# A fused attention-and-MLP kernel: reordering the second and third row chunk of its first phase

## The chip, the cores and the metric

The kernel runs on one core of one Trainium2 chip. The metric is the device time of one execution in microseconds (us). Engines are named as the profile names them: PE (TensorE, matmuls), PEld (its weight loads), DVE (VectorE), ACT (ScalarE), POOL (GpSimd), SP (SyncE, which here issues most transfers).

## The reference

For 2048 rows of width 512, the result mixes a linear attention `a` and an MLP `b` by a gate. All of it is float32.

```python
x = A_x                                              # 1 x 2048 x 512
g = sigmoid((x * gate_w).sum(-1, keepdims=True))
qkv = x @ wqkv                                       # 32 heads of 16
pq, pk = q @ w_phi[h], k @ w_phi[h]                  # per head, 16 x 16
phi = concat([softmax(p), softmax(-p)], -1)          # features, 32 per head
kv = einsum("bhsf,bhsd->bhfd", phi_k, v)             # summed over all rows
z  = einsum("bhsf->bhf", phi_k)
a  = ((phi_q @ kv) / (phi_q . z + 1e-6)) @ wo
h  = x @ w1 + b1                                     # 1376 hidden
b  = (h * tanh(softplus(h))) @ w2
out = g * a + (1 - g) * b
```

## The kernel before, in words

**Precision.** A float32 product is made of three products of split operands: each operand is written as a high part (rounded to PE's fp32r) and a low part (operand minus high part). ScalarE makes the high part by a copy, VectorE or GpSimd makes the low part by a subtraction. So every weight and every block of x costs a copy and a subtraction, and every matmul group is `xh·wh`, `xh·wl`, `xl·wh`.

**Stages.** A start stage multiplies the per-head matrices `w_phi` into the K and Q weights (`fuse`, into PSUM) and splits the results into `wkh`, `wkl`, `wqh`, `wql` (`fsplit`, L806); `raw_k` (L821) also copies the unsplit K weights out, since differences of them are needed later. The K products of the first chunk are woven into this stage (`k_part`, L813). Phase A then goes through the 2048 rows in 8 chunks of 256 rows (`a_ops`, two tiles of 128 rows each). Phase B does the MLP and the rest of the attention in 4 blocks of 512 rows.

**A chunk of phase A.** `k`, `v`, `q` are PE's groups of 12 matmuls a tile. VectorE turns K into features: `mx` and `mn` (largest and smallest of each head), `d0` and `d1` (two subtractions into the tile `E`), then ScalarE's exponential `E`, then VectorE's sum `S`, reciprocal `rS` and multiplication `ml` (L292). `ve` and `qe` are ScalarE's evictions of V and Q, `st` stores Q's projection. `z` adds the features into a sum in DRAM by an accumulating transfer on GpSimd's queue. `kv` (L455) multiplies the features with V and adds into one PSUM tile for all chunks; it needs `ml` and `ve` of both tiles. `xh` and `xl` split x of the next chunk, `ldx` loads x of the chunk after that.

**Fast chunks.** Chunks 3 and 4 counted from 0 (the fourth and fifth) use fewer products, made of sums of weights (`t1` to `t4`, L301) and sums of x (`sa`, split by `sh` and `sl`). The sums of weights are split by the steps `h0` to `h3` (ScalarE) and `l0` to `l3` (GpSimd, `l2` VectorE). In a fast chunk `ca` (L376) adds two products in PSUM on VectorE before the group `s4` continues it. The names `H`, `O`, `L` with a number are the copy, subtraction and load of a piece of the MLP's weights.

**Order.** Nothing is scheduled by the compiler around these steps: every engine does its instructions in the order of the program. That order is written by hand as strings, one for each chunk: `FIRST`, `SECOND` and `BEFORE` for chunks 0, 1 and 2, `SEVEN` for the fast ones, and so on. `run` (L209) takes the names one after another and issues each step on its engine. A plain name is a step of the chunk itself, `'` one of the chunk before, `+` one of the chunk after, `#` a weight step. Each engine has its own queue, so the order in a string matters only between steps of one engine, and through the waits between engines.

**Buffers.** The feature tiles `E` have 4 buffers, V tiles (`io`) 4, x in raw form (`tx`) 2, split x (`hl`) 8 half-tiles. PSUM has 3 tiles for K and Q (`a`), 4 for V and others (`dn`), one for `kv`. A step that takes a buffer waits until its last reader is done.

Of the kernel before, what the change touches and what calls it, by code (L numbers as in the profile page):

```python
# [34 lines left out]
FAST = range(3, 5)  # L35
# [6 lines left out]
    S0 rS0 ml0 S1 rS1 ml1 q0 qe0 st0 q1 qe1 st1  # L42
"""
SECOND = """
    h0# h1# l0# h3# l1# l3# z0' z1' k0 xh mx0 mn0 d00 d10 xl ldx k1 E0 L0# L1# mx1 mn1 d01 d11 v0 E1 S0 rS0 ve0 ml0 t2# h2# z0
    v1 S1 rS1 ml1 ve1 q0 qe0 st0 q1 qe1 st1 l2# kv' kv
"""
BEFORE = """
    k0 z1' xh xl sa mx0 mn0 d00 d10 ldx k1 E0 H0# O0# L2# mx1 mn1 d01 d11 v0 E1 sh0 sl0 S0 rS0 ve0 ml0 z0
    v1 H1# O1# L3# S1 rS1 ml1 ve1 q0 qe0 st0 q1 sh1 sl1 qe1 st1  # L50
"""
SEVEN = """
# [46 lines left out]
def tile_gated_mix(ctx: ExitStack, tc: tile.TileContext, xT, wv, wkT, wqT, bd, w1a, w1b, b1, w2a, w2b, wo, out):  # L99
# [10 lines left out]
    def mm(*a, **k):  # L110
        return pin(nc.tensor.matmul(*a, **k))  # L111
# [8 lines left out]
    def k4(name, tag, dt=F32):  # L120
        return T([P, 1024], dt, tag, {"E": 4, "tx": 2, "oh": 2, "z": 1}[tag], name)

    def k2(name, tag, dt=F32):
        return T([P, 512], dt, tag, {"pq": 3, "io": 4, "hl": 8}[tag], name)
# [5 lines left out]
    def act(out_, in_, fn=AF.Copy, **k):  # L130
        return pin(A_.activation(out_, in_, fn, **k))  # L131
# [7 lines left out]
    def f32(ap):  # L139
        return ap.bitcast(F32)  # L140
# [65 lines left out]
    def at(key, name, fn):  # L206
        steps.setdefault((key, name), []).append(fn)
# [32 lines left out]
    def proj(x, t, wh, wl, tag):  # L240
        ps = psum("proj", tag)
        xh, xl = x
        sl = slice(t * P, (t + 1) * P)
        n = 0
        for a, w in ((xh, wh), (xh, wl), (xl, wh)):
            for k in range(KT):
                mm(ps, a[k // 2][:, k % 2, sl], w[:, k, :], start=(n == 0), stop=(n == 3 * KT - 1))
                n += 1
        return ps
# [10 lines left out]
    def feat_ops(key, t, src, d, negative=False):  # L260

        n = str(t)

        def red(name, op):
            d[name] = T([P, H], F32, name, 2, name)
            pin(V.tensor_reduce(d[name], hv(src()), axis=AX.X, op=op))

        def dd(a):
            if "E" not in d:
                d["E"] = k4("E", "E")  # L270
            E = hv(d["E"][:, a * 512 : (a + 1) * 512])
            if (a == 0) != negative:
                pin(V.tensor_sub(E, hv(src()), d["mx"][:, :, None].to_broadcast([P, H, DH])))
            else:
                ins = pin(V.tensor_sub(E, d["mn"][:, :, None].to_broadcast([P, H, DH]), hv(src())))  # L275
                if key == ("B", 0) and t == 1:
                    last[0] = ins

        def ss():
            d["S"] = T([P, 2 * H], F32, "Sm", 2, "Sm")  # L280
            pin(V.tensor_reduce(d["S"], hv(d["E"][:, :]), axis=AX.X, op=ALU.add))  # L281

        at(key, "mx" + n, lambda: red("mx", ALU.max))
        at(key, "mn" + n, lambda: red("mn", ALU.min))
        at(key, "d0" + n, lambda: dd(0))
        at(key, "d1" + n, lambda: dd(1))
        at(key, "E" + n, lambda: act(d["E"], d["E"], AF.Exp))
        at(key, "S" + n, ss)
        at(key, "rS" + n, lambda: pin(V.reciprocal(d["S"], d["S"])))

    def scale_by(d, eng):
        pin(eng.tensor_mul(hv(d["E"][:, :]), hv(d["E"][:, :]), d["S"][:, :, None].to_broadcast([P, 2 * H, DH])))  # L292
# [96 lines left out]
    def a_ops(c):  # L389
        key = ("A", c)  # L390
        P_ = psA[c] = {}
        for t in range(2):
            d = {}
            Es[c, t] = d

            def k_(t=t):
                P_["k", t] = proj(xs[c], t, wkh, wkl, "a")

            def v_(t=t):
                P_["v", t] = proj(xs[c], t, wvh, wvl, "dn" if c or t else "kv")  # L400

            def q_(t=t):
                P_["q", t] = proj(xs[c], t, wqh, wql, "a")

            def ve(t=t):
                vs[c, t] = k2("v", "io")
                act(vs[c, t], P_["v", t])

            def qe(t=t):
                P_["qs", t] = k2("qs", "pq")  # L410
                act(P_["qs", t], P_["q", t])

            def qa(t=t):
                P_["qs", t] = k2("qs", "pq")
                pin(V.scalar_tensor_tensor(P_["qs", t], P_["q", 0], -1.0, P_["m7s"], op0=ALU.mult, op1=ALU.subtract))

            def st(t=t):
                i = 2 * c + t
                pin(Sy.dma_start(pqd[i * P : (i + 1) * P, :], P_["qs", t]))

            at(key, f"v{t}", v_)
            if c not in FAST:
                at(key, f"k{t}", k_)
                at(key, f"q{t}", q_)
            at(key, f"ve{t}", ve)
            if t and c in FAST:
                at(key, "qa", qa)
            else:
                at(key, f"qe{t}", qe)
            at(key, f"st{t}", st)  # L430
            feat_ops(key, t, lambda t=t: P_["k", t][:, :], d, t == 1 and c in FAST)
            at(key, f"ml{t}", lambda d=d: scale_by(d, V))

            def zs(t=t, d=d):
                if c >= NCH - 2:
                    end = c == NCH - 1
                    for sl in (slice(0, 512), slice(512, 1024)) if end and t else (slice(0, 1024),):
                        ins = pin(G_.tensor_add(Z["acc"][:, sl], Z["acc"][:, sl], d["E"][:, sl]))
                        if end and not sl.start:
                            tc.add_manual_dep(ins.ins, last[t].ins.name, SYNC, reason="VectorE's own sums first")  # L440
                elif c:
                    pin(G_.dma_start(zd[t][:, :], d["E"], accum_op=ALU.add))
                else:
                    pin(G_.dma_start(zd[t][:, :], d["E"]))

            at(key, f"z{t}", zs)
        if c == NCH - 2:
            def zld():
                Z["acc"] = k4("zacc", "z")
                pin(Sy.dma_start(Z["acc"], zd[0][:, :]))  # L450

            at(key, "zld", zld)
            at(key, "za", lambda: pin(G_.dma_start(Z["acc"], zd[1][:, :], accum_op=ALU.add)))

        def kv():  # L455
            if not kvs:
                kvs.append(psum("kvp", "kv")[:, : NG * 64].rearrange("p (g f) -> p g f", g=NG))
            (kvp,) = kvs
            for t in range(2):
                E, v = Es[c, t]["E"], vs[c, t]  # L460
                Ev = E[:, :].rearrange("p (a r b x) -> p b r a x", a=2, r=2, b=8)
                for u in range(8):
                    for r in range(2):
                        o = (u % 2) * 64 + 32 * r
                        mm(kvp[o : o + 32, u // 2, :], v[:, u * 64 + 32 * r : u * 64 + 32 * r + 32], Ev[:, u, r, :, :],
                           start=(c == 0 and t == 0 and u < 2), stop=(c == NCH - 1 and t == 1), skip_group_check=True)

        odd = c + 1 - c % 2
        if odd + 1 in FAST:
            at(("A", odd + 1), "kk", kv)  # L470
        else:
            at(key, "kv", kv)
        if c in FAST:
            fast_ops(c, key, P_)
        if c + 1 in FAST:
            fast_operands(c + 1, key)
        if c + 1 < NCH:
            def xh():
                new_x(c + 1)
                for j in range(2):  # L480
                    x_hi(c + 1, j)

            at(key, "xh", xh)
            for j in range(2):
                at(key, "xl", lambda j=j: x_lo(c + 1, j, V if c else G_))
        if c + 2 < NCH:
            at(key, "ldx", lambda: ldx(c + 2))
# [318 lines left out]
    def fsplit(h, l, k):  # L806
        act(h[:, k, :], acc[k])
        pin(V.tensor_sub(l[:, k, :], acc[k], f32(h[:, k, :])))
# [4 lines left out]
    def k_part(k):  # L813
        for t in range(2):
            sl = slice(t * P, (t + 1) * P)
            if t not in pk:
                pk[t] = psum("proj", "a")
            for n, (a, w) in enumerate(((xs[0][0], wkh), (xs[0][0], wkl), (xs[0][1], wkh))):
                mm(pk[t], a[k // 2][:, k % 2, sl], w[:, k, :], start=(k == 0 and n == 0), stop=(k == KT - 1 and n == 2))

    def raw_k(k):  # L821
        act(wkr[:, k, :], acc[k])
# [7 lines left out]
    fsplit(wkh, wkl, 1)  # L830
    acc[2] = fuse(skT, 2)
    fsplit(wkh, wkl, 2)
    raw_k(0)
    raw_k(1)
    k_part(0)
    acc[3] = fuse(skT, 3)
    fsplit(wkh, wkl, 3)
    k_part(1)
    for j in range(2):
        h, l = [w[:, 2 * j : 2 * j + 2, :].rearrange("p k f -> p (k f)") for w in (wvh, wvl)]  # L840
# [99 lines left out]
```

## Time and profile before

| | |
|---|---|
| median of 3 runs | 457.06 us (456.77 to 458.35) |
| the profiled execution | 457.48 us |
| its span, first to last instruction | 455.6 us |
| PE, DVE, ACT, POOL busy | 444.9, 318.3, 207.1, 153.7 us |
| granted TensorE clock, mean | 0.996 |

The profile page is that of one execution. Its waits name the engine whose event came last; a timeline row gives the start, the duration, the engine, the line, what is written from what, how many instructions are merged into the row and, in brackets, the idle time before it with what ended it. Helper lines such as L111 (matmul) and L131 (ScalarE) stand for many steps, so rows are told apart by tiles: `proj<-wkh,xh` is a K group, `wvh` V, `wqh` Q. The tiles named `th`, `tl`, `sh`, `sl` written from `wkr` or `wqr` are the split sums of weights. The third chunk's K group starts at 54.18 us, the fourth chunk's first group at 71.62 us.

### The profile page before, as it was taken

Reading aid. Unit: us, or ns where it says so; the run is one execution under the profiler, and the core shown is the slowest. Engines: PE = TensorE matmul, PEld = TensorE weight load, DVE = VectorE, ACT = ScalarE, POOL = GpSimd, SP = SyncE. Lnnn points to the kernel's source line nnn. Section 1 sums busy time; section 2 is a strip of 40 time slices with the busy share of each in tenths; the row PEclk is TensorE's granted clock in tenths of the full one; section 3 lists DMA queues with packets and bytes.
Section 4 is the critical chain, followed back from the end, with each engine's and each line's share of the span. In section 5 each row is a group of like instructions: output and inputs, shape, how many; then the busy total and the mean of one; then the engine's idle time right before and its main releaser. Section 6 shows DMA issues by size and latency. Waiting matters only on the chain.

```text
span 455.6 us, 7013 instructions
## 1 busy us (share of the span) xinstructions
PE 444.9 (98%) x2760; PEld 363.6 (80%) x2760; DVE 318.3 (70%) x421; ACT 207.1 (45%) x286; POOL 153.7 (34%) x110
## 2 busy tenths in 40 slices
PE   7999699999999999999999999999999999999996
PEld 7888588888888888878787887887887888787885
DVE  2498887889597999979997985666967629611002
ACT  4772443726435564636347354434254553234220
POOL 2299465845724356320213212023212122221211
PEclk9999899999999999999999999999999999999999
DMA  7413845689596300222435050431141402030002
GB/s 281 160 62 122 201 125 139 149 204 264 163 322 149 116 24 1 72 68 71 138 101 154 17 148 21 109 114 54 24 117 56 112 19 92 1 81 13 1 0 94
DMA packets 27609, 47.41 MB, mean 104 GB/s; under 512 B 5940, under 2 KB 14132, under 8 KB 27576
## 3 DMA queue, kind: packets, MB, share of 16 engines
q1 hardware_dynamic: 25528, 39.88, 28.5%
q0 software_dynamic: 1904, 6.82, 7.8%
q8 instruction: 22, 0.36, 0.3%
q10 hardware_dynamic: 144, 0.26, 0.2%
q14 instruction: 11, 0.09, 0.1%
HBM read 23.87 MB, written 14.69 MB: 85 GB/s over the span
## 4 chain that ended last, share of the span: by engine, by line
PE 87%; DVE 0%; ACT 0%; issue 0%
PE up L111 27%; PE down L111 26%; PE proj L111 21%; PE wo L111 10%; PE num L111 2%; PE kvp L111 2%; DVE io L784 0%; ACT qs L131 0%; PE z L111 0%; ACT xh L131 0%; PE kvT L603 0%
## 5 line engine op out<-in xcount | busy, mean ns | idle before, releaser
L649 POOL TENSOR_TENSOR l<-act,h 128x512 fp32r<-128x512 f32 x44 | 61.4, 1397 | 219.1 <-ACT h L131 183.4
L131 ACT ACTIVATE act<-up,b1s 128x512 f32<-128x512 f32 x44 | 30.3, 688 | 88.6 <-PE up L111 88.5
L131 ACT ACTIVATE E<-E 128x1024 f32<-128x1024 f32 x32 | 33.6, 1060 | 55.6 <-DVE E L275 37.7
L292 DVE TENSOR_TENSOR E<-E,Sm 128x1024 f32<-128x1024 f32 x32 | 46.6, 1457 | 1.0
L281 DVE TENSOR_REDUCE Sm<-E 128x64 f32<-128x1024 f32 x32 | 38.7, 1211 | 4.9 <-ACT E L131 4.9
L111 PE MATMUL wo<-woh,ohl 128*128 128x512 f32 x128 | 40.8, 389 | 0.0
L111 PE MATMUL down<-w2ah,h 128*128 128x512 f32 x96 | 37.5, 390 | 0.0
L111 PE MATMUL down<-w2ah,l 128*128 128x512 f32 x96 | 37.4, 389 | 0.0
L111 PE MATMUL down<-w2al,h 128*128 128x512 f32 x96 | 37.3, 389 | 0.0
L784 DVE SCALAR_TENSOR_TENSOR io<-down,og_sb,io 128x512 f32<-128x512 f32 x16 | 11.1, 749 | 31.0 <-PE down L111 31.0
L111 PE MATMUL down<-w2bh,h 128*128 128x512 f32 x80 | 31.2, 390 | 0.0
L111 PE MATMUL down<-w2bl,h 128*128 128x512 f32 x80 | 31.1, 389 | 0.0
L111 PE MATMUL down<-w2bh,l 128*128 128x512 f32 x80 | 31.1, 389 | 0.0
L131 ACT ACT_TABLE_LOAD x20 | 25.7, 1283 | 10.4 <-PE up L111 10.1
L758 DVE TENSOR_TENSOR ohl<-num,ohl 128x512 fp32r<-128x512 f32 x16 | 10.2, 679 | 26.4 <-ACT ohl L131 26.4
L131 ACT ACTIVATE h<-act 128x512 fp32r<-128x512 f32 x44 | 27.8, 632 | 1.4
L111 PEld LDWEIGHTS wo<-woh,ohl 128*128 128x128 f32 x128 | 24.0, 188 | 5.1
L111 PE MATMUL up<-xbh,w1ah 128*128 128x512 f32 x96 | 26.2, 394 | 0.0
L111 PE MATMUL up<-xbh,w1al 128*128 128x512 f32 x96 | 25.7, 389 | 0.0
L111 PE MATMUL up<-xbl,w1ah 128*128 128x512 f32 x96 | 25.7, 389 | 0.0
L111 PE MATMUL wo<-wol,ohl 128*128 128x512 f32 x64 | 24.9, 389 | 0.0
L546 DVE TENSOR_TENSOR xbl<-xraw,xbh 128x1024 fp32r<-128x1024 f32 x8 | 10.0, 1288 | 19.8 <-ACT xbh L131 19.8
(156 smaller groups left out, 1006.0 us busy)
## 6 DMA issues: line engine op xcount, KB each, us to landing
xraw<-in_xT_dram SPq DMA_DIRECT2D x16, 512.0 KB, 5.4
eT<-tt SPq DMA_DIRECT2D x128, 64.0 KB, 2.0
zd<-E POOLq DMA_DIRECT2D x12, 512.0 KB, 6.6
pqd<-qs SPq DMA_DIRECT2D x16, 256.0 KB, 3.3
pq<-pqd SPq DMA_DIRECT2D x16, 256.0 KB, 2.9
out_dram<-io SPq DMA_DIRECT2D x16, 256.0 KB, 2.1
raw<-in_w1a_dram SPq DMA_DIRECT2D x3, 512.0 KB, 4.6
raw<-in_w2a_dram SPq DMA_DIRECT2D x3, 512.0 KB, 4.5
```

The lines of the kernel that those rows point to most:

```text
L111: return pin(nc.tensor.matmul(*a, **k))
L131: return pin(A_.activation(out_, in_, fn, **k))
L281: pin(V.tensor_reduce(d["S"], hv(d["E"][:, :]), axis=AX.X, op=ALU.add))
L292: pin(eng.tensor_mul(hv(d["E"][:, :]), hv(d["E"][:, :]), d["S"][:, :, None].to_broadcast([P, 2 * H, DH])))
L546: last[h] = pin(V.tensor_sub(xb[b][1][:, :, sl], kt(raw[h], SC), f32(xb[b][0][:, :, sl])))
L649: pin(G_.tensor_sub(U[i]["l"], U[i]["a"], f32(U[i]["h"])))
L758: pin(V.tensor_sub(ohl[h, gp][:, 512:], num[h, gp], f32(ohl[h, gp][:, :512])))
L784: pin(V.scalar_tensor_tensor(io[t], dn[t], og_sb[:, i : i + 1], io[t], op0=ALU.mult, op1=ALU.add))
```

## The change

Four edits, all to the order in which steps are issued:

1. The `kv` products of chunks 0 and 1 stood at the end of chunk 1's string. They now stand in chunk 2's string behind its first K group `k0`, as `kk` (the condition in `a_ops` now also sends chunks 0 and 1 there, as it did chunks 2 and 3 to chunk 4).
2. In chunk 1, `xh` and `xl` of the next x stand later: `xh` behind the exponential of tile 0, `xl` behind `ml0`. `ldx` stands ahead of both. `t2` moves from the middle of the string to its end, behind `ml1`.
3. The split steps `h3`, `l1`, `l3` and `h2`, `l2` of the weight sums move from chunk 1 to chunk 2. In chunk 2, `xh` and `xl` stand ahead of `k0`, and `sa`, `ldx` behind the exponential of tile 0.
4. In the start stage the raw copies of the first two K weight blocks stand behind the split of the fourth block.

```diff
 SECOND = """
-    h0# h1# l0# h3# l1# l3# z0' z1' k0 xh mx0 mn0 d00 d10 xl ldx k1 E0 L0# L1# mx1 mn1 d01 d11 v0 E1 S0 rS0 ve0 ml0 t2# h2# z0
-    v1 S1 rS1 ml1 ve1 q0 qe0 st0 q1 qe1 st1 l2# kv' kv
+    h0# h1# l0# z0' z1' k0 mx0 mn0 d00 d10 ldx k1 E0 L0# L1# xh mx1 mn1 d01 d11 v0 E1 S0 rS0 ve0 ml0 xl z0
+    v1 S1 rS1 ml1 ve1 q0 qe0 st0 q1 qe1 st1 t2#
 """
 BEFORE = """
-    k0 z1' xh xl sa mx0 mn0 d00 d10 ldx k1 E0 H0# O0# L2# mx1 mn1 d01 d11 v0 E1 sh0 sl0 S0 rS0 ve0 ml0 z0
+    z1' xh xl k0 kk h3# l1# l3# mx0 mn0 d00 d10 k1 E0 sa ldx h2# mx1 mn1 d01 d11 v0 E1 H0# O0# L2# l2# S0 rS0 ve0 ml0 sh0 sl0 z0
     v1 H1# O1# L3# S1 rS1 ml1 ve1 q0 qe0 st0 q1 sh1 sl1 qe1 st1
 """
...
         odd = c + 1 - c % 2
-        if odd + 1 in FAST:
+        if odd < FAST[-1]:
             at(("A", odd + 1), "kk", kv)
         else:
             at(key, "kv", kv)
...
     fsplit(wkh, wkl, 2)
-    raw_k(0)
-    raw_k(1)
     k_part(0)
     acc[3] = fuse(skT, 3)
     fsplit(wkh, wkl, 3)
+    raw_k(0)
+    raw_k(1)
     k_part(1)
```

More of the change, by code (lines that the diff above doesn't have):

```diff
@@ L44 @@
 SECOND = """
-    h0# h1# l0# h3# l1# l3# z0' z1' k0 xh mx0 mn0 d00 d10 xl ldx k1 E0 L0# L1# mx1 mn1 d01 d11 v0 E1 S0 rS0 ve0 ml0 t2# h2# z0
-    v1 S1 rS1 ml1 ve1 q0 qe0 st0 q1 qe1 st1 l2# kv' kv
+    h0# h1# l0# z0' z1' k0 mx0 mn0 d00 d10 ldx k1 E0 L0# L1# xh mx1 mn1 d01 d11 v0 E1 S0 rS0 ve0 ml0 xl z0
+    v1 S1 rS1 ml1 ve1 q0 qe0 st0 q1 qe1 st1 t2#
 """
 BEFORE = """
-    k0 z1' xh xl sa mx0 mn0 d00 d10 ldx k1 E0 H0# O0# L2# mx1 mn1 d01 d11 v0 E1 sh0 sl0 S0 rS0 ve0 ml0 z0
+    z1' xh xl k0 kk h3# l1# l3# mx0 mn0 d00 d10 k1 E0 sa ldx h2# mx1 mn1 d01 d11 v0 E1 H0# O0# L2# l2# S0 rS0 ve0 ml0 sh0 sl0 z0
     v1 H1# O1# L3# S1 rS1 ml1 ve1 q0 qe0 st0 q1 sh1 sl1 qe1 st1
```

## The prediction

> **What bounds the kernel now.** I read the page first, then the waits of PE over the whole run, then PE's timeline around the longest wait, then the timelines of the engines that feed it.
>
> ```profile
> PE 444.9 (98%) x2760; PEld 363.6 (80%) x2760; DVE 318.3 (70%) x421; ACT 207.1 (45%) x286; POOL 153.7 (34%) x110
> ```
>
> PE (TensorE) carries the kernel: 98% busy. A change that removes no matmul can only win PE's holes. The list of PE's waits is the list of all that can be won:
>
> ```profile
> PE kvp L111 <- ACT xh L131: 3.5, 1, 3.5
> PE fuse L111 <- DMA bds<-in_bd_dram: 1.8, 1, 1.8
> PE warm L111 <- DVE ones L179: 1.1, 1, 1.1
> PE kvp L111 <- DVE E L292: 0.6, 1, 0.6
> ```
>
> Two are the start of the program. The other two (3.5 and 0.6) lie in one place, the `kv` products at the end of the second chunk. PE's timeline there (start, duration, what, idle before it):
>
> ```profile
> 46.40 1.07 PE L111 MATMUL proj<-wqh,xl 128*128 128x512 f32 x4
> 47.40 1.10 PE L111 MATMUL kvp<-E,v 128*32 128x64 f32 x64
> 49.06 0.65 PE L111 MATMUL kvp<-E,v 128*32 128x64 f32 x32 [0.56 <-DVE E L292]
> 53.17 1.08 PE L111 MATMUL kvp<-E,v 128*32 128x64 f32 x32 [3.46 <-ACT xh L131]
> 54.18 2.08 PE L111 MATMUL proj<-wkh,xh 128*128 128x512 f32 x4
> ...
> 60.74 1.07 PE L111 MATMUL proj<-wvh,xh 128*128 128x512 f32 x4
> ```
>
> The second chunk's last Q group starts at 46.40. The first chunk's 64 `kv` products follow, then the second chunk's: its second half waits 3.46 us. Then the clock is lost too: 32 products take 1.01 us from start to start where 64 took little more, and the third chunk's first four K products 1.87 (54.18 until the next group, by the 2.08 shown) instead of 0.9. The wait is booked to ScalarE's `xh`, but see what VectorE did (xl, then mx of tile 1, S, rS and ml of tile 0, t2, and ml of tile 1):
>
> ```profile
> 39.48 4.06 DVE L258 TENSOR_TENSOR xl<-xraw,xh 128x512 fp32r<-128x512 f32 x2 [1.51 <-ACT xh L131]
> 43.47 0.68 DVE L266 TENSOR_REDUCE mx<-proj 128x32 f32<-128x512 f32 x1
> ...
> 45.86 1.21 DVE L281 TENSOR_REDUCE Sm<-E 128x64 f32<-128x1024 f32 x1
> 47.10 0.55 DVE L289 RECIPROCAL Sm<-Sm 128x64 f32<-128x64 f32 x1
> 47.69 1.23 DVE L292 TENSOR_TENSOR E<-E,Sm 128x1024 f32<-128x1024 f32 x1
> 48.83 1.22 DVE L310 SCALAR_TENSOR_TENSOR wqr<-wkr,wqr 128x1024 f32<-128x1024 f32 x1
> ...
> 51.80 1.23 DVE L292 TENSOR_TENSOR E<-E,Sm 128x1024 f32<-128x1024 f32 x1
> ```
>
> ml of tile 0 ends at 48.92 and PE goes on at 49.06; ml of tile 1 ends at 53.03 and PE goes on at 53.17: 0.14 both times. So the features (ml1), not `xh`, end the hole. VectorE lost 1.51 us waiting for the split of x and 4.06 on two subtractions ahead of mx1.
>
> **The change part by part.**
>
> *kv of both chunks behind the third chunk's first K group.* No product is added or removed: 128 `kv` products run as one batch behind `k0`. Their price is seen where the kernel already does this, in the fifth chunk:
>
> ```profile
> 89.39 1.99 PE L111 MATMUL kvp<-E,v 128*32 128x64 f32 x128
> 91.31 0.73 PE L111 MATMUL proj<-wkh,xh 128*128 128x512 f32 x2
> ```
>
> From 89.39 to 91.31 is 1.92 us. Entering such a batch costs 0.09 (46.40 to 47.40 is 1.00 for four products that otherwise take 0.91), leaving it about 0.12 (0.73 for a pair against 0.61 for a pair elsewhere). A K group is 12 products at 0.227 (0.91 for four), 2.72. So from the end of Q at 47.31 to the first V product of the third chunk: 2.72 + 0.09 + 1.92 + 0.12 + 2.72 = 7.57, which puts it at 54.88. Before it started at 60.74. **Gain 5.86 us**, of which 4.0 is idle time and the rest the slow clock.
>
> The slow clock's share here is 1.84 us by rows (5.86 less 0.56 and 3.46 of idling). The Trainium skill, page "TensorE: Matmul & The Clock Gate", section "Part 1: The HAM clock gate", has the array at half rate after an idle window of about 3.4 us, until about as long a stretch of work has passed. By that page the loss is half of 3.4, an estimate of 1.7, and the time 0.1 higher than by rows; the 3.46 us hole followed by a slow stretch, and the 0.56 hole not, agree with it.
>
> That holds if nothing new is late. `k0` of the third chunk needs only its x, so the batch's last quarter is wanted at 47.31 + 2.72 + 0.09 + 3/4 of 1.92 = 51.56.
>
> *Features ahead of x's low parts, `xh` behind E0.* VectorE stood free from 37.97 (39.48 less 1.51). Now mx1, mn1, d01, d11 run there: four operations in 2.39 (43.47 to 45.86), to 40.4. S 1.24, rS 0.59, ml 1.14 of tile 0 (45.86, 47.10, 47.69, 48.83) to 43.3; xl at its free price, 0.6 a half by the 0.68 operations' spacing, to 44.5 (x is wanted by PE from 47.3); S, rS, ml of tile 1 to 47.5. So ml1 comes 4 us before it is wanted. t2 follows (1.14) to 48.6. On ScalarE `xh` of chunk three now runs behind E0; until 43.3 nothing but xl would want it. `ldx` of chunk four moves ahead of `xh` and xl but stays between the same neighbours on SP's queue (stores of the first chunk, weight pieces): nothing.
>
> *h3, l1, l3 and h2, l2 a chunk later.* On POOL, l0 keeps its place, l1 and l3 leave; the two sum transfers z0', z1' move up behind l0:
>
> ```profile
> 37.78 2.41 POOL L313 TENSOR_TENSOR tl<-wkr,th 128x1024 fp32r<-128x1024 f32 x1
> 40.14 2.85 POOL L313 TENSOR_TENSOR tl<-wqr,th 128x1024 fp32r<-128x1024 f32 x1
> 42.95 2.85 POOL L313 TENSOR_TENSOR sl<-wkr,sh 128x1024 fp32r<-128x1024 f32 x1
> 45.74 1.14 POOL L444 DMA_DIRECT2D zd<-E  x2
> ...
> 55.45 1.42 POOL L330 TENSOR_TENSOR sraw<-xraw 128x256 f32<-128x256 f32 x2 [1.03 <-DVE xl L258]
> ```
>
> They issue at 40.2 instead of 45.74, so the E buffers that the third chunk reuses come free sooner. POOL then idles until ml1, issues z1' at about 48.1 and does l1 and l3 from 48.7 to 54.0 (2.41 + 2.85), then the four sums `sa`. Behind l1 and l3 are queued `sa`, and with it the load of chunk five's x, and the low parts that the fourth chunk wants. On ScalarE h3 stands ahead of the third chunk's E0, which waits for VectorE anyway.
>
> This gives the one new collision. The row 39.48 shows it: xl's halves, at 0.55 to 0.6 each when free, took 4.06; the first ends as l0 ends (40.19) plus 0.55, the second as l1 ends (42.99) plus 0.55, at 43.54. Two-input operations in SBUF wait here for POOL's whole instruction. In the new order it is xl of chunk four that meets l1 and l3. ScalarE splits that x after Q is evicted:
>
> ```profile
> 51.58 1.08 ACT L131 ACTIVATE qs<-proj 128x512 f32<-128x512 f32 x2
> 52.54 1.16 ACT L131 ACTIVATE xh<-xraw 128x512 fp32r<-128x512 f32 x2
> ```
>
> One eviction (half of 0.96) from about 47.5 and half the split put xl at 48.6; free it ends at 49.9, at the price of 39.48 at 52.7. mx0 of the third chunk wants VectorE when `k0` ends, 50.1, so it can slip by 2.6. No wait of PE hangs on that before the fourth chunk, whose sum `ca` (L376) PE needs for its fourth group s4:
>
> ```profile
> 68.15 5.01 DVE L292 TENSOR_TENSOR E<-E,Sm 128x1024 f32<-128x1024 f32 x1
> 75.73 1.29 DVE L258 TENSOR_TENSOR xl<-xraw,xh 128x512 fp32r<-128x512 f32 x2 [2.58 <-ACT xh L131]
> ...
> 78.14 0.69 DVE L376 TENSOR_TENSOR proj<-proj,m 128x512 f32<-128x512 f32 x1
> ```
>
> ```profile
> 79.78 0.62 PE L111 MATMUL proj<-sh,xh 128*128 128x512 f32 x2
> ```
>
> `ca` ends 0.95 us before s4 (78.83, 79.78). Shifted by 5.86, VectorE must have finished the third chunk when xl starts at 69.87, s4 at 73.92. The third chunk's second K group ends at 54.88 and holds mx1 until then; then 2.39, l2 1.14, S, rS, ml of tile 0 2.97, S and rS 1.83 and ml1 at its worst price here, 5.01: 68.3. That is 1.6 us in hand. **Cost taken: 0**; the cover is VectorE's idle 2.58.
>
> *Two raw copies behind the fourth weight split.*
>
> ```profile
> 11.84 1.08 ACT L131 ACTIVATE wkr<-fuse 128x512 f32<-128x512 f32 x2
> 13.94 0.60 ACT L131 ACTIVATE wkh<-fuse 128x512 fp32r<-128x512 f32 x1 [1.01 <-PE fuse L111]
> ```
>
> They ran in a stretch where ScalarE afterwards idled 1.01 us for PE, so the split does not come earlier; what is behind it (V weights, two more copies) comes up to 1.08 later. The chunk's K products keep PE busy meanwhile. Between 0 and a loss of 1.08 I take 0.
>
> **Sum.** The profiled execution took 457.48; less 5.86 is 451.62. The median of the runs shown is 0.42 lower, 457.06; from it 451.2, and that I forecast, since a median will be compared.
>
> **The rivals.**
>
> *VectorE gains nothing from its new order.* If ml1 of the second chunk still ended at 53.03, PE would find it at 53.17 instead of 51.56: 1.6 us idle, too short by the 0.56 and 3.46 cases to be sure of the clock, gain 4.25, time 452.8. For it speaks only that VectorE was full from 43.5 on; against, the 1.51 us and the xl collision, both gone from ahead of ml1. Chance 0.07.
>
> *The collision moves to the third chunk.* Rows 39.48 and 68.15 show two-input operations of VectorE waiting while POOL works; here each could lose every time. xl from 48.6 behind l1 and l3, 2.41 + 2.85, ends at 54.5; then 4.78 for both tiles' four operations, l2 1.14, and twice 1.83 + 5.01: 74.1. xl, mx, mn, `ca` (75.73 to 78.83) 3.1: 77.2, and s4 waits 3.3. Gain 2.6, time 454.5. Against it: ml of 47.69 took 1.23, and in chunk two the halves of xl got in between POOL's instructions. Chance 0.08 for a wait of over 1 us. The Trainium skill, "SBUF — State Buffer", section "Who interferes with whom", states the mechanism: a pair of ports that VectorE shares with GpSimd is an exclusive lock, held for the whole instruction of whoever starts first. The two ends in row 39.48 agree with that.
>
> *Slower: x of chunk five comes late.* Its load waits for `sa`:
>
> ```profile
> 58.41 0.33 SPq L156 DMA_DIRECT2D xraw<-in_xT_dram  x1
> ```
>
> ```profile
> DMA to landing us min/median/max: 3.6/7.2/11.6
> ```
>
> (The last row: the x loads up to the middle of the run.) Before, 17.3 us lay between this issue and xl at 75.73. Now `sa` ends at about 57 (54.0 and twice 1.42), up to 59.5 with a lock, and xl stands at 69.87: 10.4 to 12.9. The longest landing, 11.6, fits or misses by 1.2. It turns the sign when the landing passes about 17 us; behind a second such transfer (23.2) it would end at 82.7, 12.8 late, less 0.95 of margin, plus the slow clock again (1.9): 465. No landing of the trace is near. Chance 0.04.
>
> **How the numbers follow.** Forecast 0.81, the three rivals 0.07, 0.08, 0.04. The range runs from 450.3 (the lowest run shown less 5.86, and 0.6 for the holes' edges) to 454.2, which takes in the first rival and all but the end of the second. A measurement of this kernel tells about 0.5% (2.3 us) from no change: faster by more than that is all of the forecast, the first rival and most of the second, 0.91; within it 0.04; slower 0.05.
>
> **What would show it.** Right: no wait of PE on `kv` above 0.6 us, one batch of 128 about 50.1, V of the third chunk at about 54.9, PE's clock full from 20 to 80 us, PE's busy time lower by the slow stretch, ml1 of the second chunk ending near 47.5. Wrong: a wait in front of the batch (first rival), before s4 near 74 us (second), or ScalarE's `xh` near 69 waiting for a transfer (third).

## The result, and the profile after

The changed kernel takes 453.0 us (median of 20 runs, 452.06 to 457.75) against 457.39 for the kernel before (20 runs): a ratio of 0.9919, 95% interval 0.9899 to 0.994. It is 4.4 us faster where 5.9 was forecast. The profiled execution took 452.06 and has a span of 450.0 us (before 455.6). Three executions on record ran far longer than all others and are left out of every count: one of e11 below (747.11 us, granted clock 0.557) and two of the kernel before (637.76 and 1579.33 us).

The page of the changed kernel, PE's busy time, and the list of all of PE's waits:

```profile
PE 442.6 (98%) x2760; PEld 360.9 (80%) x2760; DVE 323.8 (72%) x421; ACT 206.8 (46%) x286; POOL 151.3 (34%) x110
```

```profile
PE fuse L111 <- DMA wT<-in_wkT_dram: 1.4, 1, 1.4
PE warm L111 <- DVE ones L179: 1.1, 1, 1.1
PE proj L111 <- DVE proj L376: 1.0, 1, 1.0
```

Both waits on `kv` are gone. A new one has come: 1.0 us for the sum `ca` (L376). PE's timeline at the place of the old hole and at the new wait:

```profile
44.55 1.07 PE L111 MATMUL proj<-wqh,xl 128*128 128x512 f32 x4
45.45 1.07 PE L111 MATMUL proj<-wkh,xh 128*128 128x512 f32 x4
46.36 1.07 PE L111 MATMUL proj<-wkl,xh 128*128 128x512 f32 x4
47.27 1.07 PE L111 MATMUL proj<-wkh,xl 128*128 128x512 f32 x4
48.27 1.99 PE L111 MATMUL kvp<-E,v 128*32 128x64 f32 x128
50.19 1.20 PE L111 MATMUL proj<-wkh,xh 128*128 128x512 f32 x4
...
53.04 1.07 PE L111 MATMUL proj<-wvh,xh 128*128 128x512 f32 x4
...
73.21 0.72 PE L111 MATMUL proj<-sh,xh 128*128 128x512 f32 x2 [0.97 <-DVE proj L376]
```

K of the third chunk follows Q of the second without a gap (45.45), `kv` runs as one batch of 128, and the granted clock is 1.00 from 18.12 to 53.04 us (before, it was 0.84 between 47 and 58).

To compare executions one must take out the start. The first chunk's first V product comes at 19.97 us in the profile before and at 18.12 here; e1 below, one profile, speaks against the change as the reason. From there, in us:

| from that product to | before | after | after less before |
|---|---|---|---|
| the third chunk's first V product | 40.77 | 34.92 | -5.85 |
| the fourth chunk's s4 | 59.81 | 55.09 | -4.72 |
| the fifth chunk's first V product | 74.19 | 70.17 | -4.02 |
| the first product of the MLP | 137.19 | 133.55 | -3.64 |

So the hole closed by 5.85 us, and 2.2 us were given back behind it: 1.13 at s4, 0.7 in the rest of the fourth chunk and the `kv` batch after it, 0.4 later. Of the 0.7, 0.26 lie where PE's last group of the fourth chunk (79.06) waits for VectorE's sum `qa` (L415, a part of Q), which ends at 79.01; the rest is spread over several rows. The 0.4 belongs to this execution: from the fifth chunk's first V product to the MLP it took 63.38 us, but 63.01 and 63.12 in two later profiles of the same kernel (e7, e12) and 63.00 before. Those two give back 1.8 and 1.9.

VectorE and POOL show why s4 waited:

```profile
44.44 1.22 DVE L292 TENSOR_TENSOR E<-E,Sm 128x1024 f32<-128x1024 f32 x1
45.58 1.22 DVE L310 SCALAR_TENSOR_TENSOR wqr<-wkr,wqr 128x1024 f32<-128x1024 f32 x1
46.85 6.12 DVE L258 TENSOR_TENSOR xl<-xraw,xh 128x512 fp32r<-128x512 f32 x2
52.90 0.68 DVE L266 TENSOR_REDUCE mx<-proj 128x32 f32<-128x512 f32 x1
...
55.29 0.68 DVE L266 TENSOR_REDUCE mx<-proj 128x32 f32<-128x512 f32 x1
...
60.65 2.77 DVE L292 TENSOR_TENSOR E<-E,Sm 128x1024 f32<-128x1024 f32 x1
...
65.17 4.98 DVE L292 TENSOR_TENSOR E<-E,Sm 128x1024 f32<-128x1024 f32 x1
70.07 1.28 DVE L258 TENSOR_TENSOR xl<-xraw,xh 128x512 fp32r<-128x512 f32 x2
...
72.47 0.68 DVE L376 TENSOR_TENSOR proj<-proj,m 128x512 f32<-128x512 f32 x1
```

```profile
46.18 0.88 POOL L442 DMA_DIRECT2D zd<-E  x1 [3.28 <-DVE E L292]
46.76 2.72 POOL L313 TENSOR_TENSOR tl<-wqr,th 128x1024 fp32r<-128x1024 f32 x1
49.11 2.70 POOL L313 TENSOR_TENSOR sl<-wkr,sh 128x1024 fp32r<-128x1024 f32 x1
...
59.93 2.41 POOL L513 TENSOR_TENSOR w1al<-raw,w1ah 128x1024 fp32r<-128x1024 f32 x1 [3.92 <-ACT w1ah L131]
...
65.12 2.70 POOL L513 TENSOR_TENSOR w1al<-raw,w1ah 128x1024 fp32r<-128x1024 f32 x1
67.47 1.59 POOL L338 TENSOR_TENSOR sl<-sraw,sh 128x512 fp32r<-128x512 f32 x1
```

ml1 of the second chunk ends at 45.66, long before it is wanted. But xl (1.28 when free, 70.07) starts at 46.85 just behind l1 at 46.76 and takes 6.12 us, the length of l1 and l3 and its own: its first half takes 5.52 and ends behind l3, its second 0.68. mx0 of the third chunk, whose K group ended at 48.2, starts at 52.90. ml0 of that chunk (60.65) meets the subtraction O0 (59.93) and takes 2.77, ml1 (65.17) meets O1 and sl1 and takes 4.98. VectorE does not stand idle again before `ca`, which ends at 73.15, when PE had wanted it at 72.08.

### The profile page after: what moved, and what is told of

It reads as the page before. It is cut to its first block, busy times and chain, and to the rows that moved or that the text cites. A ratio compares the mean times of both kernels' runs of the same rounds, so it can differ in the third digit from the quotient of the medians.

```text
span 450.0 us, 7013 instructions
## 1 busy us (share of the span) xinstructions
PE 442.6 (98%) x2760; PEld 360.9 (80%) x2760; DVE 323.8 (72%) x421; ACT 206.8 (46%) x286; POOL 151.3 (34%) x110
## 4 chain that ended last, share of the span: by engine, by line
PE 81%; DVE 5%; issue 1%; ACT 0%; DVEq 0%
PE up L111 27%; PE down L111 26%; PE proj L111 15%; PE wo L111 10%; PE num L111 2%; PE kvp L111 1%; DVE Sm L281 1%; DVE E L292 1%; DVE mx L266 1%; DVE mn L266 1%; DVE io L784 0%; DVE E L275 0%; DVE xl L258 0%; DVE E L273 0%; DVE Sm L289 0%
## 5 line engine op out<-in xcount | busy, mean ns | idle before, releaser
L649 POOL TENSOR_TENSOR l<-act,h 128x512 fp32r<-128x512 f32 x44 | 60.3, 1370 | 220.1 <-ACT h L131 183.7
L292 DVE TENSOR_TENSOR E<-E,Sm 128x1024 f32<-128x1024 f32 x32 | 48.1, 1504 | 1.0
```

What stands on the lines that cost most here:

```text
L649: pin(G_.tensor_sub(U[i]["l"], U[i]["a"], f32(U[i]["h"])))
```

## The experiments

All runs of one group stand beside runs of the kernel before on the same chip, and each ratio is to these. The groups are e1 to e4, e5 to e7, e8 and e9, e10 to e12. "Stretch" is the time in the profile from the first chunk's first V product to the first product of the MLP: 137.19 before, 133.55 in the changed kernel's profile.

**The place of the raw copies alone (e1).**

```diff
+    raw_k(0)
+    raw_k(1)
     k_part(0)
     acc[3] = fuse(skT, 3)
     fsplit(wkh, wkl, 3)
-    raw_k(0)
-    raw_k(1)
```

> The changed kernel with the two raw copies back ahead of the fourth weight split (edit 4 undone). Main theory (the copies' place is worth nothing; the earlier start of the first chunk's K products in the changed profile, 9.53 against 10.96 us, is where the weight transfers happened to land): the median stays within 0.5 us of the changed kernel's 453.0, and PE still waits about 1.0 us before the fourth group of the fourth chunk. Rival (the copies' new place brings the start forward): 1.0 to 1.9 us slower than the changed kernel, 454 to 455.

Median 452.91, ratio to before 0.9905 (0.9879 to 0.9931); stretch 133.26, first K product at 9.77, wait at s4 0.95. Edit 4 is worth nothing that shows. The first V product comes at 18.38, almost as early as with the edit (18.12), so this one profile does not make the edit the cause of the early start.

**The products alone (e2).**

```diff
-    v1 S1 rS1 ml1 ve1 q0 qe0 st0 q1 qe1 st1 l2# kv' kv
+    v1 S1 rS1 ml1 ve1 q0 qe0 st0 q1 qe1 st1 l2#
...
-    k0 z1' xh xl sa mx0 mn0 d00 d10 ldx k1 E0 H0# ...
+    k0 kk z1' xh xl sa mx0 mn0 d00 d10 ldx k1 E0 H0# ...
```

> The kernel before with edit 1 alone: kv of the first two chunks behind the third chunk's first K group, all other orders as before. Main theory (VectorE's arrival in the fourth chunk is what limits now, so the new feature order buys little beyond the moved products): ml1 of the second chunk still ends near 53, the kv batch waits 1 to 2 us for it with a full clock, the wait before the fourth group of the fourth chunk is small, and the median gains 3.5 to 4.5 us: 453 to 454, within 1 us of the whole change. Rival (the feature order carries the gain): gain of 2 us or less, 455.4 or more.

Median 452.69 (451.84 to 452.93), ratio 0.99 (0.9877 to 0.9923). PE in this kernel, and VectorE's ml1 of the second chunk:

```profile
49.63 1.55 PE L111 MATMUL kvp<-E,v 128*32 128x64 f32 x96
52.65 0.65 PE L111 MATMUL kvp<-E,v 128*32 128x64 f32 x32 [1.48 <-ACT xh L131]
53.24 1.20 PE L111 MATMUL proj<-wkh,xh 128*128 128x512 f32 x4
```

```profile
51.28 1.23 DVE L292 TENSOR_TENSOR E<-E,Sm 128x1024 f32<-128x1024 f32 x1
```

ml1 ends at 52.51 and PE goes on 0.14 later, as it did before. The batch waits 1.48 us and the granted clock stays at 1.00; there is no wait at s4; the stretch is 133.04, 4.15 less than before. Edit 1 by itself gives as much as all four, since with the old order of the subtractions nothing is given back behind the hole.

**The order alone (e3).** The changed kernel with `kv' kv` again at the end of the second chunk, `kk` gone from the third; the rest as in the changed kernel.

> The changed kernel with edit 1 undone: kv of both chunks again at the end of the second chunk. Main theory (features in the new order end with the Q products, so the hole closes either way): no wait above 0.6 us before the kv products, the same wait of about 1 us before the fourth group of the fourth chunk, median within 0.7 us of the changed kernel, 452.5 to 453.7. Rival (the K products are needed to cover the features): a wait of 2 us or more before kv, 455 or more.

Median 452.81 (451.69 to 456.68), ratio 0.9915 (0.9888 to 0.9941). The second chunk's `kv` does not wait at all and s4 waits 0.96, as expected. But the profiled execution (454.67) has a wait that was not expected, in the fifth chunk's batch. VectorE, POOL and PE of this profile:

```profile
80.55 3.50 DVE L292 TENSOR_TENSOR E<-E,Sm 128x1024 f32<-128x1024 f32 x1
80.56 2.40 POOL L513 TENSOR_TENSOR w1bl<-raw,w1bh 128x1024 fp32r<-128x1024 f32 x1
...
87.76 0.65 PE L111 MATMUL kvp<-E,v 128*32 128x64 f32 x32 [2.42 <-DVE E L292]
```

and the same two instructions in the changed kernel's profile:

```profile
80.12 1.22 DVE L292 TENSOR_TENSOR E<-E,Sm 128x1024 f32<-128x1024 f32 x1
```

```profile
80.14 3.46 POOL L513 TENSOR_TENSOR w1bl<-raw,w1bh 128x1024 fp32r<-128x1024 f32 x1
```

ml of tile 0 of the fourth chunk and POOL's O3 start within 0.02 us of each other; this near tie of two starts is called the tie below. The one that gets through first takes its free time (1.22 or 2.40), the other about the sum of both (3.46 or 3.50). The recorded starts do not tell the winner at this distance: here ml0 starts 0.01 ahead and loses, in the changed kernel 0.02 ahead and wins. When POOL wins, the features are 2.3 us late and the batch of the fifth chunk waits.

**The subtractions back into the second chunk, where POOL was idle (e4).**

```diff
-    h0# h1# l0# z0' z1' k0 ... S0 rS0 ve0 ml0 xl z0
+    h0# h1# l0# z0' z1' l1# k0 ... S0 rS0 ve0 h3# ml0 xl z0 l3#
...
-    z1' xh xl k0 kk h3# l1# l3# mx0 ...
+    z1' xh xl k0 kk mx0 ...
```

> The changed kernel with l1, h3 and l3 put back into the second chunk, into GpSimd's idle stretches there (l1 behind z1', l3 behind z0, h3 behind ve0), so that xl of the fourth chunk's x meets no GpSimd subtraction. Main theory (what was given back is the lock on xl, 6.12 us instead of 1.29, which makes the sum ca late): xl takes under 2.5 us, the third chunk's mx0 starts with the end of its first K group, PE does not wait before the fourth group of the fourth chunk, and the median is 1.2 to 2.0 us below the changed kernel: 451.0 to 451.8. Rival (VectorE's own work is the limit, wherever GpSimd works): the wait stays at 0.7 us or more and the median within 0.5 us of the changed kernel.

Median 450.4 (449.93 to 453.81), ratio 0.9867 (0.9834 to 0.9901): 2.6 below the changed kernel's 453.0, and 2.3 to 2.5 below e1 to e3 on the same chip, more than the 1.2 to 2.0 expected; one run of the six, 453.81, stands apart. All of PE's waits, and VectorE's xl and mx0 in the third chunk:

```profile
PE fuse L111 <- DMA wT<-in_wkT_dram: 1.7, 1, 1.7
PE warm L111 <- DVE ones L179: 1.1, 1, 1.1
```

```profile
49.46 1.28 DVE L258 TENSOR_TENSOR xl<-xraw,xh 128x512 fp32r<-128x512 f32 x2
50.67 0.68 DVE L266 TENSOR_REDUCE mx<-proj 128x32 f32<-128x512 f32 x1
```

xl takes 1.28, s4 no longer waits, the stretch is 131.41: 5.78 less than before. ml0 and ml1 of the third chunk still take 2.77 and 4.97 here, so without the delay of xl they do not make s4 wait. ml0 and ml1 of the second chunk pay instead (2.69 and 2.01), which had time.

**The tie in the fourth chunk (e5 to e11).** The changed kernel's runs lie in two groups, 16 at 452 to 454.3 and 4 at 456.65 to 457.75. The tie is a candidate. e5 is e4 with O3 (and the load behind it) moved to the fifth chunk; e6 is the changed kernel with ml0 behind S1 in the fourth. The edit of e5:

```diff
-        w = {3: "H2# O2# L4# H3# O3# L5#", 4: "H4# O4# L6# H5# O5# L7#"}[c]
+        w = {3: "H2# O2# L4# H3#", 4: "O3# L5# H4# O4# L6# H5# O5# L7#"}[c]
```

> The variant with l1, h3, l3 in the second chunk, and one GpSimd subtraction (O3, the low part of a w1b piece, with the load L5 behind it) moved from the fourth chunk to the fifth, where VectorE works on PSUM. In the changed kernel's profile ml of tile 0 of the fourth chunk starts at 80.12 and O3 at 80.14; in the order-only variant they start at 80.55 and 80.56, O3 wins, ml takes 3.50 us and the kv batch waits 2.4. Main theory (that near tie for the shared port makes the spread among this kernel's runs): no run above 452 us, the median 450.0 to 450.6, ml of tile 0 there under 1.6 us. Rival (the spread comes from the start or from transfers): single runs of 452.5 or more remain, as the 453.8 of the variant without this edit.

Median 451.74 (451.54 to 453.01, 4 runs), ratio 0.9878 (0.9855 to 0.9901), stretch 132.02. ml0 takes 1.22 as expected, but the median missed 450.0 to 450.6 and one run lies at 453.01, so this run does not decide about the tie. In the profile O3 in its new place starts at 85.29 and meets xl of the sixth chunk's x, which takes 4.24 from 84.30.

The edit of e6:

```diff
+        text = SEVEN.replace("more", w)
+        if c == 3:
+            text = text.replace("E1 ml0 z0", "E1").replace("v1 S1 rS1", "v1 S1 ml0 z0 rS1")
```

> The changed kernel with ml of tile 0 of the fourth chunk behind the sum S of tile 1, so that GpSimd's O3 starts first every time. Main theory (lost tie): ml takes about 2 us or more, the kv batch in the fifth chunk waits 2 us or more in the profile, and the median is 1.5 to 4 us above the changed kernel's 453.0: 454.5 to 457. Rival (the tie is not what spreads the runs, VectorE has slack there): median within 0.7 us of the changed kernel, wait below 0.7 us.

A miss: median 453.17 (452.62 to 453.43, 4 runs), the batch waits 0.6 us, no run near 456.7. ml0 stands behind S1, starts when O3 is done (83.20) and takes 1.22. The waiting was filled with S1, so the tie was taken away and not lost.

> The changed kernel itself once more, beside the two others on the same chip. Main theory: median 452.5 to 453.5, most runs between 452 and 454.3 and about one in five near 456.7; the profile, if it falls on one of these, shows the kv batch of the fifth chunk waiting over 2 us for the features. Rival (start or transfers): a profile of such a run shows PE waiting for a transfer instead.

A miss: 12 runs from 451.41 to 457.46, median 455.43, ratio 0.9945 (0.9916 to 0.9974). Six of the twelve, not one in five as expected, lie at 456.3 to 457.5, all with a mean clock of 0.995 or 0.996; six lie below 454.6, five of them with 0.998 to 1.0. The profile fell on the shortest. How much of the change's gain a series shows thus depends on how often the long runs come.

Then the tie was given away by something too small to cost anything itself, a memset of one element a partition, on VectorE ahead of ml0 (e8) or on GpSimd ahead of O3 (e9):

```diff
# e8
-    ... d01 d11 E1 ml0 z0
+    ... d01 d11 E1 nudge ml0 z0
...
+    at(("A", 3), "nudge", lambda: pin(V.memset(nudge, 0.0)))
# e9
+    at(("A", 3), "nudge", lambda: pin(G_.memset(nudge, 0.0)))
...
-        w = {3: "H2# O2# L4# H3# O3# L5#", ...
+        w = {3: "H2# O2# L4# H3# nudge O3# L5#", ...
```

> The changed kernel with one tiny memset on VectorE (128x1) ahead of ml of tile 0 of the fourth chunk: it hands the tie at about 80.1 us to GpSimd's O3 and changes nothing else. Main theory (the tie makes the changed kernel's two kinds of runs): ml takes 3 us or more, the kv batch of the fifth chunk waits 2.2 us or more, and all runs lie at 453.8 or above, at about 454.5 with a full clock and 456.5 with a clock of 0.995. Rival (chance or transfers elsewhere): runs spread as the changed kernel's, several below 453.2.

> The changed kernel with the same tiny memset on GpSimd ahead of O3: it hands the tie to VectorE. Main theory: ml takes about 1.2 us, the kv batch does not wait, all runs lie between 451.3 and 453.6 with no clock of 0.995, median 452.0 to 453.0; only the wait before the fourth group of the fourth chunk (about 1 us) is left. Rival: one run in three or five near 456.7 as for the changed kernel.

e9: 452.1 to 453.88, median 453.12, both a little above what was expected; no wait at the batch, stretch 133.22, one clock of 0.996 at 453.29. e8 is half a miss: median 453.51, and the profile shows the wait again (2.4, PE's waits below) and a stretch of 135.67, but three of six runs lie below 453.2. The memset took 0.06 us, and ml0 and O3 start at the same recorded time; in those three runs VectorE seems to have won all the same, though no profile fell on one.

```profile
PE kvp L111 <- DVE E L293: 2.4, 1, 2.4
PE fuse L111 <- DMA bds<-in_bd_dram: 1.7, 1, 1.7
PE warm L111 <- DVE ones L179: 1.1, 1, 1.1
PE proj L111 <- DVE proj L377: 1.0, 1, 1.0
```

```profile
80.49 3.49 DVE L293 TENSOR_TENSOR E<-E,Sm 128x1024 f32<-128x1024 f32 x1
80.49 2.41 POOL L514 TENSOR_TENSOR w1bl<-raw,w1bh 128x1024 fp32r<-128x1024 f32 x1
```

Last, five memsets of four elements instead of one memset: on GpSimd in e4's kernel (e10), on VectorE in the changed kernel (e11).

> The variant with l1, h3, l3 in the second chunk, and five tiny memsets on GpSimd ahead of O3 in the fourth chunk, which hand the tie there to VectorE. Main theory (the two locks together are all that the change gives back): PE has no wait after the start, the stretch from the first chunk's first V product to the first MLP product is 131.2 to 131.7 us against 133.55 in the changed kernel's profile, the median is 449.8 to 450.6 and no run is above 451.5. Rival (something else spreads the runs): runs of 452 or more remain.

> The changed kernel with five memsets on VectorE ahead of ml of tile 0 of the fourth chunk, so that GpSimd's O3 starts first in every run. Main theory: ml takes 3 us or more, the kv batch of the fifth chunk waits 2.4 to 2.8 us, every run lies at 453.8 or above, some at 454.5 with a full clock and some at 456.5 with a clock of 0.995, where the hole has also cost the clock. Rival (the runs near 456.7 have another cause): all runs near 454.5, or some still below 453.2.

e10: 449.98 to 451.14, median 450.66, ratio 0.9856 (0.9833 to 0.9879), stretch 131.35, nothing in PE's waits but the start; ml0 starts 0.71 us ahead of O3. The median is 0.06 above the expected span. e11: its profile fell on the execution of 747.11 us, so that ml0 lost in the others is taken from their times and not seen. These eleven lie at 453.81 to 455.12 (five, clock 0.995 to 1.0) and 456.93 to 457.84 (six, clock 0.992 to 0.996). Ratio 0.9976 (0.9953 to 0.9999). With VectorE held back, no run is below 453.8 and nearly the whole gain is gone; with GpSimd held back, and xl clear of l1 and l3, the spread is 1.2 us. Of the changed kernel's 34 runs (the result, e7 and e12) ten lie above 456; of the eleven of e9 and e10, none; of the eleven of e11, six. This speaks for the tie as the cause of the long runs, and e11 goes against its rival as stated. It is not shown in a trace of a long run.

> The changed kernel once more, for a profile of one of its long runs if one comes. Main theory: a run of 456 to 457.5 shows the kv batch of the fifth chunk waiting over 2 us and a slow stretch of PE's clock behind it; a run of 451.4 to 453.6 shows neither. Rival: a long run shows PE waiting elsewhere.

Two runs, 452.65 and 452.71; stretch 133.27, s4 waits 1.0, the batch does not. No long run was caught, so where the clock falls in one has not been seen in a trace.

## Why the prediction was right or wrong

**The hole: right, to 0.01 us.** 5.86 was worked out and 5.85 came, to the third chunk's first V product. Its sub-steps hold too: ml1 was forecast for 47.5 in the times of the profile before, which is 45.65 after the 1.85 us of earlier start, and it ended at 45.66; the batch ran as 128 products at 48.27 (forecast 48.25); the clock stayed full. That the hundredths agree is luck, since the sum is made of rows rounded to a few hundredths. e10 shows the whole of it at the end of the stretch: 137.19 less 131.35 is 5.84.

**The release of the hole: right.** ml1 and not `xh` ended it, though the wait is booked to `xh`; e2 shows the same label with the same wait for ml1. The first rival, VectorE gaining nothing from its order, did not come, since the order did what it should. e2, where ml1 does come late, puts its price to the test: 1.6 us of waiting and a gain of 4.25 were worked out, 1.48 and 4.15 measured.

**"Cost taken: 0" for the collision: wrong.** This is the step that failed. Two of its terms were too small. xl of the fourth chunk's x was priced at 4.06 at worst, from the row of chunk two, where its halves got in between l0 and l1; here it took 6.12, with its first half behind both l1 and l3. And ml of tile 0 was priced free (1.14) where it took 2.77. mx1 of the third chunk so started 2.3 us later than the forecast's floor, and ml1 ended at 70.15 where 66.45 was forecast in the times of this profile: 3.7 late. The forecast had 1.6 us in hand and 0.95 between `ca` and s4; what these did not cover, 1.15, became a wait of 0.97. By these numbers either delay alone (2.3 or 1.6) would have stayed inside the 2.55, and e4, with only ml0's left, has no wait.

The second rival named mechanism, place and consumer, and had 3.3 us of waiting. It priced ml0 at 5.01; with the 2.77 measured, its sum gives 1.06, and 0.97 came. That is just under the "over 1 us" to which it gave its chance of 0.08, and 0.08 was far too small: the prediction's own times put xl at 48.6 and l1 at 48.7, and a row that shows a lock twice is reason to expect it. (The chance of 0.91 for "faster" counts 0.03 of this rival and not most of it; nothing else hangs on that.) The measured 453.0 lies between the forecast's 451.2 and this rival's 454.5.

The Trainium skill, page "SBUF — State Buffer", section "Who interferes with whom", says that the order of issue decides who blocks. The trace agrees for l1 (46.76) against xl (46.85). It does not for l3, which starts at 49.11 and goes ahead of the xl that has stood since 46.85; and in the fourth chunk's tie ml0 lost in e3 with a recorded start 0.01 us earlier. What decides in these cases no run here shows.

**The tie in the fourth chunk: not seen.** The forecast looked at the fourth chunk only up to s4. Behind it, in the profile before, ml of tile 0 stood at 85.80 and O3 at 85.82, as close as after, and VectorE won. A profile of one execution shows one outcome of such a tie. Whether the kernel before loses it too, and whether its own spread of 455.7 to 459.2 comes from there or from its hole, was not tried.

**Raw copies, late x of chunk five: right.** e1 shows nothing for the first; the third rival did not come, ScalarE's split of that x stood at 67.39 without waiting for a transfer.

**The number.** The median of 453.0 stands against 451.2: 1.8 off, or 4.4 gained for 5.86. The profiles account for 1.8 to 2.2 given back where the tie is won; where it is lost, e3 shows a wait of 2.42 more. The profiled execution, 452.06, came near the forecast of 451.62 for it by luck: 1.85 us of its 5.42 are the early start. Luck has a part in the median too: 4 of its 20 runs were long. In e7 it was 6 of 12, and that median, 455.43, lies outside the range of 450.3 to 454.2.

## What to carry to other kernels

A hole on the busiest engine could be priced here from its neighbours' rows alone. What then decided was whether the next engine arrives in time behind it: sum its slack with every collision lost, through to the next place where the busy engine reads its result. Where operations of VectorE and GpSimd that have delayed each other in the trace start within a few hundredths of a microsecond, one profile shows one outcome, and the times of many executions can fall in groups: order such pairs, or move one of them where it meets nothing (e5 moved it to where it met something else). Moving work out of GpSimd's idle stretch into VectorE's busy one undid part of a good change here. One edit of the four gave as much as all of them (452.69). The version with the subtractions left where GpSimd was idle took 450.4 us (e4), and with the tie ordered, on another chip, 450.66, with no run as long as e4's 453.81.

## What the runs showed of the hardware

One instruction on VectorE can lose to two on GpSimd in a row: ml1 of the third chunk, 1.22 us when free, took 4.97 to 5.00 in the profiles of the changed kernel and of every experiment but e11. A hole of 2.42 us left PE's granted clock at 1.00 in the two profiles that caught it (e3, e8), and so did one of 1.48 (e2), where one of 3.46 was followed by a slow stretch before. Among the eleven executions of e11, six had a mean clock of 0.992 to 0.996 and took about 3 us more than the five others (0.995 to 1.0). In the profile before, a mean of 0.996 goes with 1.84 us lost; by that, an estimate, the clock would be the larger part of these 3 us and not all of them. The Trainium skill, "TensorE: Matmul & The Clock Gate", section "What's actually happening", has the array at half rate after an idle window of about 3.4 us. The three shorter holes with a full clock agree. The six executions of e11 are not explained by it, if their hole was near 2.4 us; no trace of such a run was caught, and the cause stays open. And the start varies by itself: in the three profiles of the changed kernel alone (the result, e7, e12) the first chunk's first V product came between 17.78 and 18.92 us, over all profiles but e11's up to 19.97. PE waits there for a first transfer, 1.3 to 1.9 us in a piece; what else moves the start was not traced.
